# Rows of modes by way of DRAM instead of by identity products, and one slot per pair for the second weights

## The chip, the cores and the metric

One Trainium2 chip, of which the kernel uses one core. The core has TensorE (PE: matrix products into PSUM), VectorE (DVE), ScalarE (ACT), GpSimd (POOL) and SyncE (SP); POOL, SP and ACT can issue DMAs, and 16 DMA engines carry them. The metric is the device time of one execution in microseconds (us), lower is better.

## What is computed

Eight samples of 3264 positions with 192 channels. A causal convolution of seven taps per head comes first; its result, u0 here, is the input of a spectral layer that keeps the 64 lowest modes. Cut to what matters:

```python
def _attn_ref(x, weight):            # x (8, 3264, 192), weight (8 heads, 7)
    w = softmax(weight)              # over the taps
    return conv_per_head(zero_pad_left(x, 6), w)

def _moe_ref(x, w_r, w_i, w_ch):     # x: the result above
    X = np.fft.rfft(x, axis=1)
    Y[:, :64] = X[:, :64] @ (w_r + 1j * w_i)      # one 192x192 matrix per mode
    y = np.fft.irfft(Y, n=S, axis=1)
    u = x + y
    return u + np.maximum(u @ w_ch, 0.0)
```

## The kernel before

**First stage.** POOL's queue loads x, one pair of samples after the other (line 166, 177; float32 in DRAM, bf16 in SBUF), then w_ch (284, 286), then the weights of the modes in 16 groups of four modes (`load_w`, line 292), each group as two DMAs. Four pairs of samples q = 0 to 3 go through the convolution (`conv_pass`), a fold and a DFT as matrix products (`dft`), and a transpose of the spectrum (`xtrans`) to columns of modes, `xt`. The convolved rows stay in SBUF in `xall`; their transposes `ct` are made on the side (`trans_banks`).

**Mixing.** For each group g of four modes, `mix(g)` makes twelve products with the group's weights. Two groups make a step d = g // 2. `mix_copy(d)` copies the mixed spectrum of a step out of PSUM into one of two buffers `ymix`, in rows (mode of four, real or imaginary, sample). `mix_trans(d)` transposes it on PE and copies it to `yet`: 192 channels on partitions (128 and, a second time, the last 64), one column per mode and part, for each sample b. The last two groups have their own copies (lines 798 and 808), since everything after waits for them.

**Second stage.** For rows of modes, two things are wanted for each sample: the spectrum itself and the spectrum times w_ch. With those, the time signal is a product with a table `gtab` (modes by positions). Before, one set of products gives both, since the weight tiles `wa` and `wb` hold w_ch in their first 192 columns and an identity in the next 192: `yet` times that is 384 columns, spectrum times w_ch and spectrum. The result is scaled by `ascale` (2/S, and 1/S for mode 0) and kept in `zw[:, 0]` and `zw[:, 1]`. For the first pair of samples `zw_even` and `zw_odd` (lines 535 and 543) do this at once; for samples 2 to 7 each has a place in the list of slots.

The list of slots is the order of the second stage. An item (q, kk) is 256 positions of both samples of a pair; it has two slots, a = 0 and 1, of 128 positions. 52 items make 104 slots. A slot has one of eight PSUM banks (NZ = 8, slot s in bank s % 8) and goes through: C products (`ct` times w_ch, three of 192 columns on each half of the array's rows), a g product (`gtab` times `zw[:, 0]`, 384 columns on each half), a clamp at zero on ScalarE (`relu`, line 658), a y product (`gtab` times `zw[:, 1]`, 384 columns on each half) onto the clamped values, and an add of the convolved rows on VectorE (`finish`, line 679) into an output buffer. When both slots of an item are added, SP issues the store (line 699). Products that use 64 rows of the array run beside those of the other half; on one bank the halves take turns (`product`). A slot (None, b) is not an item: its products are those of the second weights of sample b, and `second_weights` (line 666) copies them to `zw`. The C products of the first five slots (`c_ahead`) and of ten others (`pairs`, "held" slots here) are made during the mixing; the held ones are parked in SBUF and brought back by ScalarE (`restore`, line 644).

**Order.** All orders of instructions are fixed when the program is built. `second_stage` (line 710) plays the stage through with assumed costs (`TAKES`, `TURN`, `SEEN`, `LOAD`) and writes PE's, ScalarE's and VectorE's instructions in the order that comes out.

**Output buffers.** `NO` buffers take the results of the first 16 items (`LATE`) in turn; six lie in `arena`, where weights lay before, and a seventh in `band`, the table of the convolution. Later items use six more in the part of `xall` that is done with. `relu` of an item waits for the stores of the item that had its buffer before (`before`, `wait_for`).

Of the kernel before, what the change touches and what calls it, by code (L numbers as in the profile page):

```python
# [19 lines left out]
def kernel(  # L20
# [9 lines left out]
    nc = tc.nc  # L30
# [58 lines left out]
    spare = sb("spare", [NK - 4, 2 * D], F32)  # L89
    ymix = [sb(f"ymix{i}", [2, D], BF16) for i in range(2)]  # L90
    bd3 = band[:, :].rearrange("p (h c) -> p h c", h=H)
    ctw = [ct[:, q, :, :, :].rearrange("p k t c -> p (k t c)") for q in range(NQ)]
# [7 lines left out]
    def wbuf(g):  # L100
# [137 lines left out]
    nc.vector.memset(ascale[:], 2.0 / S)  # L238
    nc.vector.memset(ascale[0:1, :], 1.0 / S)

# [35 lines left out]
    for u in units[6:8]:  # L276
        load_unit(*u)
    nc.gpsimd.memset(wa[:, D:2 * D], 0.0)
# [5 lines left out]
    nc.gpsimd.dma_start(out=wa[:, 0:D], in_=moe_w_ch[0:P, :])  # L284
    for i in range(2):
        nc.gpsimd.dma_start(out=wb[64 * i:64 * i + 64, 0:D], in_=moe_w_ch[P:D, :])


    NG = MODES // 4
    LAST = NG // 2 - 1  # L290

    def load_w(g):
        if g < NG:
            m0 = 8 * (g // 2) + g % 2
# [188 lines left out]
    def mix_bank(g):  # L483
        return sums[(g // 2 + (g == NG - 1)) % 2]

    def mix(g):
        yp = mix_bank(g)[:, D * (g % 2):D * (g % 2) + D]
        for j in range(3):
            for p4 in range(4):
                m = 8 * (g // 2) + g % 2 + 2 * p4  # L490
                nc.tensor.matmul(yp[32 * p4:32 * p4 + 2 * B, :], xt[:, j, :, m],  # L491
                                 wbuf(g)[:, p4, j, :], start=(j == 0), stop=(j == 2),
                                 tile_position=(0, 32 * p4), skip_group_check=True)
        if g >= NWC:
            load_w(g + NWA)

    def mix_copy(d):
        nc.scalar.copy(out=ymix[d % 2][:], in_=sums[d % 2][:, 0:2 * D].rearrange("p (g d) -> p g d", g=2))

    def mix_trans(d, groups=(0, 1), banks=None, parts=((0, B),)):  # L500

        ets = [((banks[t] if banks else ye[d % 2])[:, :].bitcast(BF16)[:, 2 * P * t:2 * P * (t + 1)]).rearrange(
            "p (g k) -> p g k", g=2) for t in range(2)]
        g0, ng = groups[0], len(groups)
        for t in range(2):
            for g in groups:
                nc.tensor.transpose(ets[t][:, g, :], ymix[d % 2][:, g, 64 * t:64 * t + P], ident[:])
        for b0, b1 in parts:
            for t in range(2):
                rows = slice(64 * t, P)  # L510
                dst = yet[rows, t, b0:b1, :].rearrange("p b (r c j) -> p r c b j", r=2, c=2)[
                    :, g0:g0 + ng, :, :, 4 * d:4 * d + 4]
# [9 lines left out]
    def scaled(dst, srcv, engine, rows=slice(0, P)):  # L522
        if engine == "v":
            return nc.vector.tensor_scalar(out=dst, in0=srcv, scalar1=ascale[rows, 0:1], scalar2=None, op0=ALU.mult)
        return nc.scalar.activation(out=dst, in_=srcv, func=ACT.Copy, scale=ascale[rows, 0:1])


    zfirst = ymix[(LAST + 1) % 2]

    def zw_part(o, i, t, modes=slice(0, P)):  # L530
        for k, w in enumerate((wa, wb)):
            nc.tensor.matmul(o, yet[:, k, i, modes], w[:, D * t:D * t + D], start=(k == 0),  # L532
                             stop=(k == 1), skip_group_check=True)

    def zw_even():

        r = slice(0, 64)
        o = ye[1][r, P:P + 2 * D]
        for i in range(2):
            zw_part(o[:, D * i:D * i + D], i, 0, r)  # L540
        scaled(zfirst[r, :, :], o.rearrange("p (i d) -> p i d", i=2), "a", r)

    def zw_odd():
        r = slice(64, P)
        w, y = (sums[0][:, 0:D], ye[0][:, 2 * P:2 * P + D]), ye[1][:, P:P + 2 * D]
        for i in range(2):
            zw_part(w[i], i, 0)
        for i in range(2):
            zw_part(y[:, D * i:D * i + D], i, 1)
        for i in range(2):  # L550
            scaled(zfirst[r, i, :], w[i][r, :], "av"[i], r)
        scaled(zw[:, 1, 0:2, :], y.rearrange("p (i d) -> p i d", i=2), "v")

# [31 lines left out]
    def pieces(s, row, which):  # L585
        n, a = slots[s]
        r = slice(64 * row, 64 * row + 64)
        if n is None:
            sides = ((0, wa),) if row == 0 else ((0, wa), (1, wb))
            return [(slice(0, 2 * D), yet[r, t, a, :], w[r, :]) for t, w in sides]  # L590
        q, kk = items[n]
        t = 2 * kk + a
        if which == "c":
            return [(slice(D * i, D * i + D), ct[r, q, blk, t, :], w[r, 0:D])
                    for blk, w, i in ((0, wa, 0), (1, wa, 1), (2, wb, row))]
        z = zw[r, 1 if which == "y" else 0, 2 * q:2 * q + 2, :] if q or which == "y" else zfirst[r, :, :]
        return [(slice(0, 2 * D), gtab[r, t, :], z.rearrange("p b d -> p (b d)"))]
# [68 lines left out]
    def second_weights(s, engine):  # L666
        q, i = divmod(slots[s][1], 2)
        copy = scaled(zw[:, :, 2 * q + i, :], Z[s % NZ][:, 0:2 * D].rearrange("p (t d) -> p t d", t=2), engine)
# [38 lines left out]
    HEAD = (-300, 330, 1500)  # L707
    TAKES = {"clamp": (930, 1150), "add": (1120, 1340), "copy": (1200, 1450), "restore": (950, 1200)}

    def second_stage():  # L710
# [30 lines left out]
        while left:  # L741
# [9 lines left out]
            if kind == 0:  # L751
# [5 lines left out]
                else:  # L757
# [6 lines left out]
            product(s, row, piece, row == 0 and k == 0 and s >= NC and slots[s] not in kept,  # L764
                    n is None and row == 1 and k == 1)
            free[row] = t + piece[0].stop - piece[0].start
# [7 lines left out]
            elif n is None:  # L774
                e = "a"
                second_weights(s, e)
# [17 lines left out]
    for g, beside in enumerate((0, 1, 1, 2, 2, 2, 1, 2, 2, 2, 2, 2, 2, 2, 0, 0)):  # L794
        d = g // 2
        mix(g)
        if g == NG - 2:
            nc.scalar.copy(out=ymix[d % 2][:, 0, :], in_=mix_bank(g)[:, 0:D])
            Z += hand_out("left", "out", (1, 1, 1, 1))
# [7 lines left out]
        elif g == NG - 1:  # L807
            nc.vector.tensor_copy(out=ymix[d % 2][:, 1, :], in_=mix_bank(g)[:, D:2 * D])  # L808
            g_ahead(range(2))
# [49 lines left out]
```

## Time and profile before

| | us |
|---|---|
| median of 3 runs (lowest, highest) | 176.18 (176.15, 177.23) |
| the profiled execution | 175.63 |
| its span, first to last instruction | 173.8 |
| busy in the span: PE | 149.3 (86%) |
| weight loads of PE | 126.5 (73%) |
| VectorE | 125.3 (72%) |
| ScalarE | 121.2 (70%) |
| GpSimd | 64.4 (37%) |

In the rows of the profile PE is the matrix product, PEld its weight load, SPq and POOLq the queues that issue DMAs. `outleft`, `sumright` and `mixright` are the PSUM banks of the second stage. A row of a group has the line of the kernel, engine, operation, output and inputs, the count, and durations. A row of the chain or of the timeline begins with its start and its length in us. A clamp is ScalarE at line 658, an add VectorE at line 679, a store SP at line 699. Of a DMA, "to landing" is the time from its issue until its data are there.

### The profile page before, as it was taken

The page shows a single profiled execution, that of the slowest core. Times are in us where ns is not written, and L with a number is a line of the kernel's source. Part 1 is how long each engine was busy: PE and PEld are TensorE (multiplying, and loading weights), DVE is VectorE, ACT ScalarE, POOL GpSimd, SP SyncE. Part 2 cuts the span into 40 slices and gives each one's busy share as a digit, 9 for nine tenths or more (in the row PEclk, how much of TensorE's full clock was granted, in tenths as well). Part 3 has the DMA queues.
Part 4 walks back from the last instruction along what each step waited for, and adds up shares of the span by engine and source line. Part 5 has one row for each costly group of instructions (what it writes and reads, how often), then busy time and mean ns, then how long its engine had stood idle before and what let it go on. Part 6 is the DMA issues. An engine that isn't in the chain of part 4 may idle for free.

```text
span 173.8 us, 6637 instructions
## 1 busy us (share of the span) xinstructions
PE 149.3 (86%) x2837; PEld 126.5 (73%) x2837; DVE 125.3 (72%) x244; ACT 121.2 (70%) x228; POOL 64.4 (37%) x106
## 2 busy tenths in 40 slices
PE   0043897899999998799998999999999999999980
PEld 0042796789889887677875754788999998999950
DVE  3892878466868868675555461597999998999990
ACT  6368365668686685665765663799989989988850
POOL 7977999877775474344244200000000000000000
PEclk9999699999999999999999999999999999999997
DMA  2999999999999999999999993088799999989995
GB/s 14 170 184 190 192 188 191 191 190 192 191 190 191 196 209 204 206 210 203 206 207 206 207 203 57 6 330 304 287 350 385 346 344 367 342 295 341 397 358 203
DMA packets 50594, 40.16 MB, mean 231 GB/s; under 512 B 29060, under 2 KB 50564, under 8 KB 50564
## 3 DMA queue, kind: packets, MB, share of 16 engines
q0 software_dynamic: 36208, 19.67, 82.3%
q1 hardware_dynamic: 14084, 19.87, 31.4%
q8 instruction: 22, 0.36, 0.8%
q10 hardware_dynamic: 272, 0.20, 0.3%
q14 instruction: 8, 0.07, 0.1%
HBM read 39.33 MB, written 20.05 MB: 342 GB/s over the span
## 4 chain that ended last, share of the span: by engine, by line
DMA 43%; PE 34%; POOL 15%; issue 3%; DVE 2%; POOLq 0%; DVEq 0%
DMA xall<-in_x_dram 18%; PE outleft L612 17%; DMA arena<-in_moe_w_i_dram 12%; DMA ct<-in_moe_w_i_dram 12%; POOL xall L166 11%; PE sumright L612 8%; PE mixright L612 8%; DVE arena L679 1%; POOL ct L296 1%; POOL loose L262 1%; PE sumright L491 1%; POOL wa L262 0%; POOL arena L296 0%; PE mixright L532 0%; DVE ymix L808 0%
## 5 line engine op out<-in xcount | busy, mean ns | idle before, releaser
L315 PEld LDWEIGHTS <-band 128*64 128x64 bf16 x944 | 38.0, 118 | 18.4 <-ACT band L233 11.0
L612 PEld LDWEIGHTS <-ct 64*128 64x128 bf16 x624 | 40.5, 94 | 5.9 <-PE trleft L612 0.5
L612 PE MATMUL outleft<-mixa,gtab 64*128 64x384 bf16 x186 | 41.9, 323 | 0.0
L315 PE MATMUL cvleft<-xall,band 128*64 128x192 bf16 (+4 forms) x640 | 29.9, 242 | 13.9 <-ACT band L233 11.0
L166 POOL DMA_DIRECT2D xall<-in_x_dram x48 | 35.9, 760 | 7.6 <-DMA xall<-in_x_dram 6.1
L612 PEld LDWEIGHTS <-gtab 64*128 64x128 bf16 x416 | 30.2, 94 | 3.4 <-PE sumright L612 0.9
L612 PE MATMUL outleft<-wa,ct 64*128 64x192 bf16 x196 | 29.9, 243 | 0.0
L344 DVE TENSOR_TENSOR arena<-xall 128x1536 bf16<-128x1536 bf16 (+1 forms) x28 | 22.4, 841 | 7.8 <-ACT xall L339 7.5
L339 ACT CAST xall<-cvleft 128x768 bf16<-128x768 f32 (+3 forms) x29 | 21.4, 756 | 9.1 <-PE cvleft L315 8.5
L658 ACT ACTIVATE outleft<-outleft 128x384 f32<-128x384 f32 x54 | 24.7, 475 | 3.3 <-PE sumright L612 0.8
L612 PE MATMUL sumright<-mixa,gtab 64*128 64x384 bf16 x88 | 26.2, 323 | 0.1
L612 PE MATMUL mixright<-mixa,gtab 64*128 64x384 bf16 x90 | 26.3, 322 | 0.0
L612 PE MATMUL outleft<-wb,ct 64*128 64x192 bf16 x98 | 21.7, 243 | 0.0
L391 DVE COPY ct<-trleft 128x1024 bf16<-128x1024 bf16 (+1 forms) x19 | 12.4, 662 | 12.1 <-PE trleft L422 7.2
L679 DVE TENSOR_TENSOR arena<-outleft,xall 128x384 f32<-128x384 f32 x35 | 18.5, 554 | 2.6 <-PE outleft L612 2.1
L315 PE MATMUL cvright<-xall,band 128*64 128x192 bf16 (+4 forms) x304 | 15.7, 245 | 2.1 <-DVE xall L337 1.5
L612 PE MATMUL mixright<-wa,ct 64*128 64x192 bf16 x96 | 17.0, 243 | 0.0
L389 ACT COPY ct<-trleft 128x1024 bf16<-128x1024 bf16 x13 | 13.2, 1013 | 4.6 <-PE trleft L419 2.5
L339 ACT CAST xall<-cvright 128x768 bf16<-128x768 f32 (+3 forms) x13 | 9.8, 751 | 7.9 <-PE cvright L315 5.5
L612 PE MATMUL sumright<-wa,ct 64*128 64x192 bf16 x84 | 14.8, 243 | 0.0
L419 PEld LDWEIGHTS <-xall 128*128 128x128 bf16 x208 | 11.7, 98 | 2.6 <-issue 0.3
L658 ACT ACTIVATE mixright<-mixright 128x384 f32<-128x384 f32 x25 | 11.8, 480 | 1.7 <-PE mixright L612 0.5
(146 smaller groups left out, 284.2 us busy)
## 6 DMA issues: line engine op xcount, KB each, us to landing
out_dram<-arena SPq DMA_DIRECT2D x25, 384.0 KB, 3.6
xall<-in_x_dram POOLq DMA_DIRECT2D x48, 192.0 KB, 7.6
out_dram<-xall SPq DMA_DIRECT2D x18, 384.0 KB, 4.1
ct<-in_moe_w_r_dram POOLq DMA_DIRECT2D x8, 288.0 KB, 9.8
ct<-in_moe_w_i_dram POOLq DMA_DIRECT2D x8, 288.0 KB, 10.5
arena<-in_moe_w_r_dram POOLq DMA_DIRECT2D x8, 288.0 KB, 9.8
arena<-in_moe_w_i_dram POOLq DMA_DIRECT2D x8, 288.0 KB, 10.7
out_dram<-band SPq DMA_DIRECT2D x4, 384.0 KB, 4.3
```

What stands on the lines that cost most here:

```text
L166: nc.gpsimd.dma_start(out=xall[:, q, t % 2, k:k + 4, :], in_=src)
L262: nc.gpsimd.affine_select(out=dst, in_=dst, compare_op=ALU.not_equal, fill=fill, base=base, pattern=pattern, channel_multiplier=1)
L296: nc.gpsimd.dma_start(out=wbuf(g)[64 * half:64 * half + 64, :, :, :], in_=src[m0:m0 + 7:2, :, :].rearrange("m (p j) e -> p m j e", j=3))
L315: nc.tensor.matmul(o, bd3[:, h, c0:c0 + P - 1:2], xall[:, q, t, ks:ks + n, GRP * h:GRP * h + GRP], start=(main and a == 0), stop=not main, ...
L339: nc.scalar.copy(out=dst, in_=srcv)
L344: nc.vector.tensor_tensor(out=cpm[:, r, :, 0:2 * nb, :], in0=src[:, :, :, 0, :], in1=src[:, :, :, 1, :], op=op)
L389: nc.scalar.copy(out=out, in_=in_)
L391: nc.vector.tensor_copy(out=out, in_=in_)
L419: nc.tensor.transpose(o, cv[:, blk, 0:P], ident[:])
L612: m = nc.tensor.matmul((Z[s % NZ] if bank is None else bank)[:, cols], l, r, start=start, stop=stop, skip_group_check=True)
L658: act = nc.scalar.activation(out=z, in_=z, func=ACT.Relu)
L679: add = nc.vector.tensor_tensor(out=o[:, :, a, :], in0=Z[s % NZ][:, 0:2 * D].rearrange("p (i d) -> p i d", i=2), in1=c_rows(q, kk)[:, a, : ...
```

## The change

- `mix_copy` and the copies of the last two groups scale at once, by 2/S, or by `ascale` for the group with mode 0; `ascale` is 1/S on the 16 rows of mode 0. They write all eight steps side by side into one buffer, `yall`, in the space of `band`; the two buffers `ymix` go.
- The steps are taken in another order, `md(d)`: 6, 7, 0, 1, 2, 3, 4, 5. The weights are loaded in that order.
- `y_rows`, new, after `zw_odd`: four DMAs on SP write the mixed spectrum from `yall` to a DRAM tile `yrows`, ordered by mode; four DMAs on POOL's queue read samples 2 to 7 back into `zy`, in rows of modes. `zy` takes the place of `zw[:, 1]`.
- The identity columns of `wa` and `wb` and the four POOL operations that made them go. `zw_odd` makes the first pair's rows of modes by products with `ident` (128 and 64 columns).
- What is left of the second weights, spectrum times w_ch, has one slot per pair: three slots with six products of 192 columns, instead of six slots with three products of 384. They stand at 11, 33 and 36 of the list (before: 12, 14, 17, 21, 68, 72). Their copies alternate between ScalarE and VectorE and do not scale.
- `NO` is 6: the output buffer in `band` goes.
- Other held slots: (18, 23), (30, 35, 43, 50), (58, 66, 74, 75), before (10, 17), (26, 30, 40, 47), (57, 63, 70, 76).

```diff
-    NO = 7
+    NO = 6
...
-    band = sb("band", [H * 2 * P], BF16)
+    band = sb("band", [max(H * 2 * P, MODES // 8 * 2 * D)], BF16)
...
-    zw = mixa[:, 0:2 * B * D].rearrange("p (t b d) -> p t b d", t=2, b=B)
-    wa = sb("wa", [2 * D], BF16)
-    wb = sb("wb", [2 * D], BF16)
+    zw, zy = [mixa[:, B * D * t:B * D * (t + 1)].rearrange("p (b d) -> p b d", b=B) for t in range(2)]
+    wa = sb("wa", [D], BF16)
+    wb = sb("wb", [D], BF16)
...
+    yall = band[:, :].rearrange("p (n g d) -> p n g d", g=2, d=D)
+    dram = ctx.enter_context(tc.tile_pool(name="dram", bufs=1, space=bass.MemoryType.DRAM))
+    yrows = dram.tile([MODES // 2, 2 * B, 2, D], BF16, tag="yrows", name="yrows")
...
-            [arena[:, OB * i:OB * (i + 1)] for i in range(NO - 1)] + [band[:, 0:OB]] +
+            [arena[:, OB * i:OB * (i + 1)] for i in range(NO)] +
...
-    nc.vector.memset(ascale[0:1, :], 1.0 / S)
+    nc.vector.memset(ascale[0:2 * B, :], 1.0 / S)
...
-    nc.gpsimd.memset(wa[:, D:2 * D], 0.0)
-    nc.gpsimd.memset(wb[:, D:2 * D], 0.0)
-    select(wa[:, D:2 * D], 1.0, 0, [[-1, D]])
-    select(wb[:, D:2 * D], 1.0, 64, [[-1, D]])
...
+    def md(d):
+        return (d + NG // 2 - 2) % (NG // 2)
...
     def mix_copy(d):
-        nc.scalar.copy(out=ymix[d % 2][:], in_=sums[d % 2][:, 0:2 * D].rearrange("p (g d) -> p g d", g=2))
+        srcv = sums[d % 2][:, 0:2 * D].rearrange("p (g d) -> p g d", g=2)
+        if md(d) == 0:
+            for g in range(2):
+                scaled(yall[:, md(d), g, :], srcv[:, g, :], g == 0, "a")
+        else:
+            scaled(yall[:, md(d), :, :], srcv, False, "a")
...
         for i in range(2):
-            zw_part(y[:, D * i:D * i + D], i, 1)
+            for k, cols in enumerate((slice(0, P), slice(P, D))):
+                nc.tensor.matmul(y[:, D * i + cols.start:D * i + cols.stop], yet[:, k, i, :],
+                                 ident[:, 64 * k:P], start=(i == 0 and k == 0), stop=True, skip_group_check=True)
...
+    def y_rows():
+        for p4 in range(4):
+            nc.sync.dma_start(out=yrows[p4:MODES // 2:4, :, :, :].rearrange("n k g d -> k n (g d)"),
+                              in_=yall[32 * p4:32 * p4 + 2 * B, :, :, :].rearrange("p n g d -> p n (g d)"))
+        for g in range(2):
+            for c in range(2):
+                r0 = 64 * g + 32 * c
+                nc.gpsimd.dma_start(out=zy[r0:r0 + 32, 2:B, :], in_=yrows[:, B * c + 2:B * c + B, g, :])
...
-    for k, b in zip((12, 14, 17, 21, 68, 72), range(2, B)):
-        slots.insert(k, (None, b))
+    for k, q in zip((11, 33, 36), range(1, NQ)):
+        slots.insert(k, (None, q))
...
-    for q, banks in ((0, (10, 17)), (1, (26, 30, 40, 47)), (2, (57, 63, 70, 76))):
+    for q, banks in ((0, (18, 23)), (1, (30, 35, 43, 50)), (2, (58, 66, 74, 75))):
...
-            return [(slice(0, 2 * D), yet[r, t, a, :], w[r, :]) for t, w in sides]
+            return [(slice(D * i, D * i + D), yet[r, t, 2 * a + i, :], w[r, :]) for i in range(2) for t, w in sides]
...
-                e = "a"
+                e = "va"[slots[s][1] % 2]
...
     zw_odd()
+    y_rows()
```

More of the change, by code (lines that the diff above doesn't have):

```diff
@@ L495, in mix, with scaled @@
             load_w(g + NWA)
-    def mix_copy(d):
-        nc.scalar.copy(out=ymix[d % 2][:], in_=sums[d % 2][:, 0:2 * D].rearrange("p (g d) -> p g d", g=2))
+    def scaled(dst, srcv, first, engine):
+        scale = ascale[:, 0:1] if first else 2.0 / S
+        if engine == "v":
+            return nc.vector.tensor_scalar(out=dst, in0=srcv, scalar1=scale, scalar2=None, op0=ALU.mult)
+        return nc.scalar.activation(out=dst, in_=srcv, func=ACT.Copy, scale=scale)
+    def mix_copy(d):
+        srcv = sums[d % 2][:, 0:2 * D].rearrange("p (g d) -> p g d", g=2)
[4 more added lines that the diff above has]
+            scaled(yall[:, md(d), :, :], srcv, False, "a")
     def mix_trans(d, groups=(0, 1), banks=None, parts=((0, B),)):
@@ L520, in mix_trans, with plain, zw_part @@
                     nc.scalar.copy(out=dst, in_=srcv)
[L522 to L530, printed above, removed]
+    def plain(dst, srcv, engine):
+        return nc.vector.tensor_copy(out=dst, in_=srcv) if engine == "v" else nc.scalar.copy(out=dst, in_=srcv)
+    def zw_part(o, b, modes=slice(0, P)):
         for k, w in enumerate((wa, wb)):
-            nc.tensor.matmul(o, yet[:, k, i, modes], w[:, D * t:D * t + D], start=(k == 0),
-                             stop=(k == 1), skip_group_check=True)
+            nc.tensor.matmul(o, yet[:, k, b, modes], w[:], start=(k == 0), stop=(k == 1), skip_group_check=True)
     def zw_even():
@@ L539, in zw_even @@
         for i in range(2):
[L540 to L541 removed]
+            zw_part(o[:, D * i:D * i + D], i, r)
+        plain(zfirst[r, :, :], o.rearrange("p (i d) -> p i d", i=2), "a")
     def zw_odd():
@@ L666, in second_weights @@
     def second_weights(s, engine):
-        q, i = divmod(slots[s][1], 2)
-        copy = scaled(zw[:, :, 2 * q + i, :], Z[s % NZ][:, 0:2 * D].rearrange("p (t d) -> p t d", t=2), engine)
+        q = slots[s][1]
+        copy = plain(zw[:, 2 * q:2 * q + 2, :], Z[s % NZ][:, 0:2 * D].rearrange("p (i d) -> p i d", i=2), engine)
         if engine == "v":
@@ L707 @@
     HEAD = (-300, 330, 1500)
-    TAKES = {"clamp": (930, 1150), "add": (1120, 1340), "copy": (1200, 1450), "restore": (950, 1200)}
+    TAKES = {"clamp": (930, 1150), "add": (1120, 1340), "copy": (960, 1200), "restore": (950, 1200)}
     def second_stage():
@@ L797 @@
         if g == NG - 2:
-            nc.scalar.copy(out=ymix[d % 2][:, 0, :], in_=mix_bank(g)[:, 0:D])
+            scaled(yall[:, md(d), 0, :], mix_bank(g)[:, 0:D], False, "a")
             Z += hand_out("left", "out", (1, 1, 1, 1))
@@ L807 @@
         elif g == NG - 1:
-            nc.vector.tensor_copy(out=ymix[d % 2][:, 1, :], in_=mix_bank(g)[:, D:2 * D])
+            scaled(yall[:, md(d), 1, :], mix_bank(g)[:, D:2 * D], False, "v")
             g_ahead(range(2))
```

28 lines of the change are left out of this document (14 added, 14 removed).

## The prediction

> **What bounds the kernel now.** I read the head of the page and its chain first, then busy time by stretches, then the chain in order of time around the joint between the two stages, and last the clamps and stores of the second stage.
>
> ```profile
> span 173.8 us, 6637 instructions
> DMA 43%; PE 34%; POOL 15%; issue 3%; DVE 2%; POOLq 0%; DVEq 0%
> ```
>
> DMA and POOL together are the first 58% of the chain, PE the rest. The stretches say why (columns: length, busy time of PE, weight loads, VectorE, ScalarE, GpSimd, clock, DMA share, GB/s):
>
> ```profile
> 8.00:10.00 2.00, 0.00 (x0) 0.00 (x0) 1.76 (x8) 0.96 (x2) 2.00 (x3) 1.00 1.53 179
> 102.00:104.00 2.00, 2.00 (x45) 1.23 (x39) 1.30 (x3) 1.47 (x3) 0.00 (x0) 1.00 1.20 205
> 106.00:108.00 2.00, 1.86 (x25) 0.79 (x23) 0.34 (x1) 0.58 (x1) 0.00 (x0) 1.00 0.10 16
> 108.00:110.00 2.00, 1.90 (x19) 1.34 (x21) 1.02 (x5) 0.68 (x3) 0.00 (x0) 1.00 0.00 0
> 112.00:113.00 1.00, 1.00 (x14) 0.57 (x10) 1.00 (x3) 1.00 (x4) 0.00 (x0) 1.00 0.03 8
> 113.00:119.00 6.00, 6.00 (x97) 5.10 (x97) 5.13 (x11) 5.73 (x14) 0.00 (x0) 1.00 0.93 349
> 160.00:166.00 6.00, 6.00 (x110) 5.55 (x108) 5.84 (x12) 4.93 (x12) 0.00 (x0) 1.00 1.01 372
> ```
>
> Up to 104 us the DMA engines are never free (share over 1, since packets overlap). From 106 to 113 they are idle: the last weights are in and no result is out. After 113 the stores fill them again, while PE and ScalarE are busy all the time. The joint in the chain of waits:
>
> ```profile
> 96.82 10.22 DMA arena<-in_moe_w_i_dram
> 107.08 0.49 PE sumright L491 x12
> 107.66 0.37 DVE ymix L808
> 108.99 0.49 PE mixright L532 x6
> ...
> 166.99 1.98 DVE arena L679 x4
> 168.99 0.56 DVE arena L679
> ```
>
> The last weight tile lands at 107.04; mixing, copying, transposing and the first pair's products follow one another until the first clamp at 110.2; then products bind until the last add at 169. PE's pace there can be read from ScalarE's clamps of the same two banks, one turn of the eight banks apart:
>
> ```profile
> 162.56 1.05 ACT L658 ACTIVATE sumright<-sumright 128x384 f32<-128x384 f32 x2
> 167.14 1.05 ACT L658 ACTIVATE sumright<-sumright 128x384 f32<-128x384 f32 x2
> ```
>
> Eight slots take 4.58 us, 0.573 us each. A slot streams 1344 columns through each half of the array (three C products of 192, one g and one y product of 384), so a column of one half costs 0.573/1344 = 0.426 ns.
>
> **The change, part by part.**
>
> *Second weights on PE.* Before, six slots hold three products of 384 columns each, one on the upper half of the array and two on the lower:
>
> ```profile
> L612 PE MATMUL sumright<-wa,yet x6: 322/322/323, 114.3 to 144.3; 64*128 64x384 bf16 x6
> L612 PE MATMUL sumright<-wb,yet x3: 323/323/323, 115.3 to 144.6; 64*128 64x384 bf16 x3
> ```
>
> After, three slots hold six products of 192. Per slot the columns are the same (384 above, 768 below, mean 576: 0.245 us), and there are three slots fewer: 3 x 0.245 = **0.74 us saved**. If only the upper half counted it would be 3 x 384 x 0.426 ns = 0.49, if the lower one 0.98. PE is busy to the end, so this lies on the path.
>
> *Their copies on ScalarE.* A scaled copy, a clamp, and (L498) a plain cast of the same size:
>
> ```profile
> 115.88 0.58 ACT L525 ACTIVATE mixa<-sumright,ascale 128x384 bf16<-128x384 f32 x1
> 116.36 0.48 ACT L658 ACTIVATE sumright<-sumright 128x384 f32<-128x384 f32 x1
> ...
> L498 ACT CAST ymix<-sumright x7: 479/480/484, 78.3 to 101.7; 128x384 bf16<-128x384 f32 x7
> ```
>
> Six of 0.58 become two of 0.48 here and one on VectorE: 2.5 us less on ScalarE, and the early held slots move from 10 and 17 to 18 and 23. ScalarE is no limit late (4.93 of 6 us) but nearly one in 113 to 119 (5.73 of 6). There PE issues 97 products where 160 to 166 has 110: at ten products per 0.573 us the 13 missing are worth 0.75 us at most. Part of the shortfall is only that the second products are wide and that held slots have no narrow ones. So 0 to 0.75; I take **0.15**, near zero.
>
> *The joint.* The first pair's products with the channel weights stay; its rows of modes now need 128 and 64 columns instead of twice 192, but they run beside the copies that the first g products wait for. Scaling moves from those copies to the mixing copy, which is on the path as well:
>
> ```profile
> 109.26 0.42 DVE L524 TENSOR_SCALAR ymix<-mixright,ascale 64x192 bf16<-64x192 f32 x1 [0.56 <-PE mixright L532]
> 107.66 0.36 DVE L808 CAST ymix<-sumright 128x192 bf16<-128x192 f32 x1 [1.91 <-PE sumright L491]
> ```
>
> One gets about 0.06 shorter, the other up to 0.06 longer: zero, with 0.1 either way. The other mixing copies get 0.10 longer each (0.58 against 0.48), and the one with mode 0 splits in two; that hides behind the weight stream (share 1.20). Uncovered it would be about 1 us. The new order of the weight tiles moves the same bytes.
>
> *GpSimd ahead of the loads.* Four operations that built the identity columns go:
>
> ```profile
> 27.51 0.34 POOL L278 MEMSET wa<- 128x192 bf16 x1
> ...
> 28.75 0.35 POOL L262 TENSOR_SCALAR_AFFINE_SELECT wb<-wb 128x192 bf16<-128x192 bf16 x1
> ...
> 52.37 0.54 POOL L284 DMA_DIRECT2D wa<-in_moe_w_ch_dram  x1 [0.27 <-DMA xall<-in_x_dram]
> ```
>
> That is 1.59 us of issuing time (27.51 to 29.10). The queue behind it is full and GpSimd later waits for it (the wait in the last row), so: zero.
>
> *The way through DRAM.* Four writes on SP and, when they have landed, four reads on GpSimd's queue. Prices, from stores:
>
> ```profile
> 112.78 5.21 SPq L699 DMA_DIRECT2D out_dram<-arena  x6
> 122.37 0.42 SPq L699 DMA_DIRECT2D out_dram<-arena  x1
> 127.92 0.45 SPq L699 DMA_DIRECT2D out_dram<-band  x1
> ...
> out_dram<-arena SPq DMA_DIRECT2D x1, 384.0 KB, 2.4
> out_dram<-band SPq DMA_DIRECT2D x1, 384.0 KB, 3.0
> ```
>
> The writes wait for VectorE's copy (108.02). Four issues of 0.42 end at 109.7; SP's next instruction, the first store, comes at 112.78, so nothing is held up. They land by 112.1 to 112.7, wholly in the idle stretch. Then GpSimd, with nothing else to do, issues four of 0.54 until about 114.6. The reads land by 117 to 118; if they took as long as the last weight tile did in a full queue (10.2), by 124.8. They are first wanted by the y product of item 13, the second item in the band buffer, stored at 127.92; its clamp starts at 124.61:
>
> ```profile
> 124.61 0.47 ACT L658 ACTIVATE mixright<-mixright 128x384 f32<-128x384 f32 x1
> ```
>
> Hence its y product waits until 125.1, and no wait shows there. What the reads do to the stores is another matter:
>
> ```profile
> q0 software_dynamic: 36208, 19.67, 82.3%
> q1 hardware_dynamic: 14084, 19.87, 31.4%
> ```
>
> A packet of q0 (543 bytes on average) takes 0.823 x 16 x 173.8 / 36208 = 63 ns of an engine, one of q1 (1411 bytes) 62 ns. The reads are 4 x 32 x 6 = 768 runs of 384 bytes: by bytes at 349/0.93 = 375 GB/s 0.79 us of all engines, by packets 768 x 63 / 16 = 3.0 us. They fall into 112.5 to 116, just as the stores fill the engines. I take 1.0, nearer to the bytes, since no row prices a lone run and part of it precedes the first store.
>
> *Six output buffers instead of seven.* The band buffer now holds the spectrum. The clamp of item n waits for the stores of item n-6 until item 15. In the trace of before, with stores landing 2.4 to 3.0 us after issue:
>
> ```profile
> 119.75 0.37 SPq L699 DMA_DIRECT2D out_dram<-band  x1
> ...
> 123.25 0.47 ACT L658 ACTIVATE sumright<-sumright 128x384 f32<-128x384 f32 x1
> 125.12 0.47 ACT L658 ACTIVATE outleft<-outleft 128x384 f32<-128x384 f32 x1
> ```
>
> Item 6 clamps at 116.36, item 0 landed at 112.78 + 2.4 = 115.2: 1.2 spare. Item 12 clamps at 123.25, item 6 landed at 122.75: 0.5 spare. Item 14 clamps at 125.12, item 8 landed at 125.4: 0.25 short. Behind a waiting clamp stand all later clamps and restores of ScalarE, and PE's y products wait for them. With stores late by 1.0 the stall is about 0.5 at item 12, some of it taken up by PE's lead: **0.4 lost**; bounds 0 and 3.0 - 0.5 = 2.5.
>
> *Sum.* -0.74 - 0.15 + 0.4 = **-0.49 us**. The profiled execution took 175.63 us (span 173.8 and 1.8 around it) and would take 175.1. The median of the runs, 176.18, is 0.55 higher; from it: 175.7.
>
> **Rivals.** *No stall, and ScalarE's relief counts.* For it: ScalarE 5.73 of 6 us busy where four of its copies stood. Against: PE's busy time shows no gap. It gives -0.98 - 0.6 = -1.6, 174.6.
>
> *The ring of six stalls in full (slower).* Mechanism: the 384-byte reads cost by the packet, push the stores of items 1 to 5 back by up to 3.0 us, and clamps 6 to 14 wait. It decides from a delay of about 1.4 us (0.5 spare plus 0.89 gained). At 2.7 the loss is 2.2, net +1.3: 177.5. For it: 63 ns whatever the packet's size. Against: 1.2 us spare in the first round, idle engines until 113. The Trainium skill, "DMA: Bandwidth & Descriptors", section Specifications, says that pieces under 512 bytes fall short of line rate, since they are read, changed and written back; by that rule the dear end, and this rival's time, would come true. The trace agrees so far as the equal 63 and 62 ns go. The same page, Queues, rings and completion order, has each DMA engine alternate between its queues packet by packet, which would put the reads between the stores rather than behind them; no run here shows both queues busy at once.
>
> *The round trip comes late.* If the reads land after 125.1, each microsecond late is one lost; the bound of 124.8 just spares it. At 2 us late: -0.89 + 2 = +1.1, 177.3.
>
> **How the numbers follow.** Forecast 0.55 (175.1 to 176.2), ScalarE's relief 0.2, the ring's stall 0.2, the late round trip 0.05. The range leaves out the far tails of both outer cases: 174.4 (all gains, -0.98 - 0.75) to 177.5. One per cent, about what a measurement of this kernel can tell from no change (its three runs spread by 0.6%), is 1.76 us. Under 174.4 lies the best of the relief and a piece of the forecast's tail, 0.14; over 177.9 the worst of the stall and the late trip, 0.12; within, 0.74.
>
> **What would show it.** Second products: eighteen of 192 columns, and the last add about 0.5 us earlier after the first clamp. The four writes within 108 to 113 and no store held up on SP. Clamps of items 6 to 15 that wait for "DMA out_dram" show the ring's price; without any, the gain is 0.9. Store landings over 4 us around 114 to 120 would show dear reads. It is wrong if PE's pace changes from 0.573, if the first clamp moves by more than 0.2, or if a y product waits for the reads.

## The result, and the profile after

The changed kernel takes 177.77 us (median of 7 runs, 177.5 to 179.05), the kernel before 176.15 (7 runs, 175.62 to 177.23). The ratio is 1.0105, 95% interval 1.0069 to 1.0140: slower by some 1.05%, where 0.3% faster was forecast, and just outside the range (177.5). The profiled execution took 177.5 us, its span 175.7. Ratios here leave disturbed executions out; in two experiments (`e5`, `e8`) it was the profiled one, so their traces are not read.

The head of the page after, with the shares of the chain by engine (those of before stand in the prediction):

```profile
span 175.7 us, 6638 instructions
DMA 47%; PE 27%; DVE 9%; POOL 9%; issue 4%; ACT 0%; POOLq 0%; DVEq 0%; ACTq 0%
```

Three spans of the trace add up to the whole: until the first clamp, from there to the end of the last add (the *stage*), from there to the end of the span (the *end*). The first clamp and the last add, after:

```profile
110.81 1.62 ACT L681 ACTIVATE outleft<-outleft 128x384 f32<-128x384 f32 x4 [0.75 <-PE outleft L635]
...
170.09 0.56 DVE L702 TENSOR_TENSOR arena<-sumright,xall 128x384 f32<-128x384 f32 x1
```

| us | first clamp | stage | end |
|---|---|---|---|
| before | 110.20 | 59.34 | 4.28 |
| after | 110.81 | 59.84 | 5.07 |

All three grew. The first is scatter: the last weight landed at 107.04 us before and at 107.76 after, and from there to the first clamp it took 3.17 before and 3.06 after. By the prediction's sum the stage should have become 0.49 shorter; it became 0.50 longer. The windows show where: five of them after (columns as in the prediction), then the three that answer in the trace of before.

```profile
114.00:118.00 4.00, 4.00 (x77) 3.59 (x74) 3.72 (x9) 3.27 (x8) 2.28 (x4) 1.00 0.87 299
116.00:118.00 2.00, 2.00 (x40) 1.81 (x36) 1.72 (x5) 1.98 (x6) 0.79 (x2) 1.00 0.88 277
118.00:122.00 4.00, 3.75 (x65) 3.16 (x61) 3.19 (x7) 3.02 (x8) 0.00 (x0) 1.00 1.06 392
122.00:126.00 4.00, 3.48 (x54) 2.71 (x51) 2.88 (x6) 2.71 (x7) 0.00 (x0) 1.00 0.98 366
160.00:166.00 6.00, 6.00 (x110) 4.82 (x108) 5.85 (x12) 4.93 (x12) 0.00 (x0) 1.00 1.06 390
```

```profile
114.00:118.00 4.00, 4.00 (x67) 3.42 (x65) 3.72 (x9) 3.88 (x9) 0.00 (x0) 1.00 1.07 398
116.00:118.00 2.00, 2.00 (x37) 1.82 (x34) 1.72 (x5) 2.00 (x5) 0.00 (x0) 1.00 1.06 396
122.00:126.00 4.00, 4.00 (x73) 3.63 (x69) 3.62 (x8) 3.69 (x10) 0.00 (x0) 1.00 0.84 308
```

From 114 to 118 the changed kernel makes 77 products against 67 (some of them narrower). From 122 to 126 it makes 54 against 73, with PE, ScalarE and VectorE all idle for a while. Late in the stage PE's pace is the same as before (110 products in six us; the row of before stands in the prediction). What ended that idle time stands in the chain in order of time:

```profile
118.83 1.03 DVE arena L702 x2
119.88 4.60 DMA out_dram<-arena
124.56 0.48 ACT outleft L681
125.09 0.32 PE outleft L635
```

The add of item 6, its store, the clamp of item 12 behind that store, and PE behind the clamp: the ring of six. Two earlier turns of it, as rows of SP's timeline, the DMA view (last number: us from issue to landing) and ScalarE's timeline:

```profile
115.33 0.37 SPq L722 DMA_DIRECT2D out_dram<-arena  x1
117.29 0.37 SPq L722 DMA_DIRECT2D out_dram<-arena  x1
...
out_dram<-arena SPq DMA_DIRECT2D x1, 384.0 KB, 4.5
out_dram<-arena SPq DMA_DIRECT2D x1, 384.0 KB, 5.3
...
119.95 1.25 ACT L681 ACTIVATE outleft<-outleft 128x384 f32<-128x384 f32 x3 [0.85 <-PE outleft L635]
122.67 0.47 ACT L681 ACTIVATE sumright<-sumright 128x384 f32<-128x384 f32 x1 [0.70 <-PE sumright L635]
```

Item 2's store is issued at 115.33 and lands at 119.86; item 8 clamps at 119.95. Item 4's, issued at 117.29, lands at 122.58; item 10 clamps at 122.67. The profile puts both waits down to PE, but a clamp that begins 0.08 us after a landing, twice, and the same for items 11 and 12, waits for the landing. In the trace of before the same two stores, issued at 114.68 and 116.56, landed 2.6 and 2.9 us after issue:

```profile
out_dram<-arena SPq DMA_DIRECT2D x1, 384.0 KB, 2.6
...
out_dram<-arena SPq DMA_DIRECT2D x1, 384.0 KB, 2.9
```

The way through DRAM, after:

```profile
108.84 1.89 SPq L570 DMA_DIRECT2D yrows<-band  x4
...
114.51 2.28 POOL L575 DMA_DIRECT2D mixa<-yrows  x4 [16.17 <-PE mixright L635]
...
yrows<-band SPq DMA_DIRECT2D x4, 96.0 KB, 3.3
mixa<-yrows POOLq DMA_DIRECT2D x4, 72.0 KB, 3.9
```

The writes landed until 113.9, so the reads were issued from 114.51, in the midst of the first stores. Their packets, 192 of them in all, moved between 116.3 and 120.5. They took 24.8% of the 16 engines' time in these 4.2 us, 1.04 us of all engines:

```profile
q0 software_dynamic: 192, 0.30, 24.8%
```

### The profile page after: what moved, and what is told of

It reads as the page before. It is cut to its first block, busy times and chain, and to the rows that moved or that the text cites. A ratio compares the mean times of both kernels' runs of the same rounds, so it can differ in the third digit from the quotient of the medians.

```text
span 175.7 us, 6638 instructions
## 1 busy us (share of the span) xinstructions
PE 149.8 (85%) x2837; PEld 125.8 (72%) x2837; DVE 124.9 (71%) x245; ACT 118.9 (68%) x225; POOL 65.2 (37%) x106
## 4 chain that ended last, share of the span: by engine, by line
DMA 47%; PE 27%; DVE 9%; POOL 9%; issue 4%; ACT 0%; POOLq 0%; DVEq 0%; ACTq 0%
DMA xall<-in_x_dram 22%; PE outleft L635 13%; DMA arena<-in_moe_w_i_dram 12%; DMA ct<-in_moe_w_i_dram 11%; POOL xall L170 7%; PE sumright L635 6%; DVE arena L702 5%; PE mixright L635 5%; DVE xall L702 4%; DMA out_dram<-arena 3%; PE sumright L494 1%; PE trleft L425 1%; POOL loose L266 1%; PE sumright L808 0%; PE mixright L522 0%
## 5 line engine op out<-in xcount | busy, mean ns | idle before, releaser
L318 PEld LDWEIGHTS <-band 128*64 128x64 bf16 x944 | 38.8, 121 | 18.6 <-ACT band L237 11.0
L318 PE MATMUL cvleft<-xall,band 128*64 128x192 bf16 (+4 forms) x640 | 30.5, 248 | 14.0 <-ACT band L237 11.0
L635 PEld LDWEIGHTS <-gtab 64*128 64x128 bf16 x416 | 29.5, 94 | 3.8 <-PE outleft L635 1.0
L635 PE MATMUL outleft<-wa,ct 64*128 64x192 bf16 x204 | 30.4, 243 | 0.0
L635 PE MATMUL sumright<-mixa,gtab 64*128 64x384 bf16 x88 | 25.4, 323 | 0.3 <-ACT sumright L681 0.2
L635 PE MATMUL mixright<-mixa,gtab 64*128 64x384 bf16 x92 | 25.5, 323 | 0.0
L635 PE MATMUL outleft<-wb,ct 64*128 64x192 bf16 x102 | 23.0, 243 | 0.0
L702 DVE TENSOR_TENSOR arena<-outleft,xall 128x384 f32<-128x384 f32 x37 | 19.7, 553 | 3.2 <-PE outleft L635 3.0
L635 PE MATMUL mixright<-wa,ct 64*128 64x192 bf16 x88 | 15.3, 242 | 0.0
L635 PE MATMUL sumright<-wa,ct 64*128 64x192 bf16 x84 | 13.9, 243 | 0.0
```

What stands on the lines that cost most here:

```text
L318: nc.tensor.matmul(o, bd3[:, h, c0:c0 + P - 1:2], xall[:, q, t, ks:ks + n, GRP * h:GRP * h + GRP], start=(main and a == 0), stop=not main, ...
L635: m = nc.tensor.matmul((Z[s % NZ] if bank is None else bank)[:, cols], l, r, start=start, stop=stop, skip_group_check=True)
L702: add = nc.vector.tensor_tensor(out=o[:, :, a, :], in0=Z[s % NZ][:, 0:2 * D].rearrange("p (i d) -> p i d", i=2), in1=c_rows(q, kk)[:, a, : ...
```

## The experiments

Each begins from the changed kernel, unless it says otherwise. Times move by some tenths between sessions, so ratios to the kernel before, run in the same session, are compared.

**Seven buffers** (`e1_ring7`): the spectrum in `band` is dead once it is written out, so the seventh buffer goes there.

```diff
-    NO = 6
+    NO = 7
...
-            [arena[:, OB * i:OB * (i + 1)] for i in range(NO)] +
+            [arena[:, OB * i:OB * (i + 1)] for i in range(NO - 1)] + [band[:, 0:OB]] +
```

> The changed kernel (177.77 us) with seven output buffers again: the seventh lies in the band space, over the spectrum that the four writes to DRAM have read by then. If the clamps of items 8, 10, 11 and 12, which begin 0.08 us after the store of the item six before has landed, are the cause, they wait no longer, PE's idle time between 120 and 126 us (some 1.5 us) goes, and the time is 176.3 (176.0 to 176.7). If PE's stall comes from the new order of the slots, or from the DMA traffic in another way, nothing changes: 177.5 to 178.0.

Measured: 177.29 us, ratio 1.0064 (1.0038 to 1.0091). Less than half of the loss went. The stage took 59.55, and clamps of items 11 and 12 still began 0.08 us after the landing of the item seven before. Neither expectation held: by the trace the ring is a cause, but with these stores seven are too few as well.

**Without the DMAs** (`e2_noroute`), six buffers:

```diff
-    y_rows()
+    nc.gpsimd.memset(zy[:, 2:B, :], 0.0)
```

> The changed kernel with six buffers, but the eight DMAs by way of DRAM left out; the rows of modes of samples 2 to 7 are set to zero instead, so their mixed spectrum is missing from the output. If the ring stalls only because the reads push the stores back by some 2 us, the first stores land 2.4 to 2.9 us after issue as before, no clamp waits for one by more than 0.3 us, and the time is 176.3 (176.0 to 176.7). If six buffers are too few on their own, it stays at 177.3 or above.

Measured: 176.73 us, ratio 1.0027 (1.0001 to 1.0054). The stage took 58.60 us, and the stores of items 2, 4 and 5 landed 2.8, 3.1 and 3.8 us after issue (4.5, 5.3 and 5.0 in the changed kernel). Item 12 alone still waited for a store, 0.4 us; the rest of the stall was gone. So the DMAs make the stores late and the ring turns it into a stall. The time stayed above the expected band because the end grew to 5.86.

**Longer runs in DRAM** (`e3_longruns`):

```diff
-    yrows = dram.tile([MODES // 2, 2 * B, 2, D], BF16, tag="yrows", name="yrows")
+    yrows = dram.tile([MODES // 8, 2, 4, 2 * B, D], BF16, tag="yrows", name="yrows")
...
-                nc.gpsimd.dma_start(out=zy[r0:r0 + 32, 2:B, :], in_=yrows[:, B * c + 2:B * c + B, g, :])
+                nc.gpsimd.dma_start(out=zy[r0:r0 + 32, 2:B, :].rearrange("p b d -> p (b d)"),
+                                    in_=yrows[:, g, :, B * c + 2:B * c + B, :].rearrange("n p k d -> n p (k d)"))
```

> The changed kernel with another layout of the DRAM tile: the writes are 1024 runs of 384 bytes (before 512 of 768), the reads 128 runs of 2304 bytes (before 768 of 384). If the reads cost by the run (63 ns each, 3.0 us of all engines), they cost 0.8 us now, the stores of items 2 to 5 land some 2 us earlier, and the time falls to 176.6 (176.2 to 177.0). If they cost by the byte, it stays at 177.5 to 178.0.

Measured: 177.61 us, ratio 1.0096 (1.0061 to 1.0131): unchanged, and the sixth store landed 5.0 us after issue, as in the changed kernel. The price is not that of short runs. The trace shows the reads as 192 packets here too. The writes, now in runs of 384 bytes, landed 2.6 to 4.1 us after issue, against 2.5 to 4.0.

**The last held slots as before** (`e4_heldend`):

```diff
-    for q, banks in ((0, (18, 23)), (1, (30, 35, 43, 50)), (2, (58, 66, 74, 75))):
+    for q, banks in ((0, (18, 23)), (1, (30, 35, 43, 50)), (2, (57, 63, 70, 76))):
```

> The changed kernel with the last held slots at (57, 63, 70, 76) as before, not (58, 66, 74, 75). In the changed kernel the last add belongs to item 49, whose store is one of 384 KB that lands 4.2 us after issue; here the last add is item 51's, whose two halves go out separately. If that end costs what the two traces show (last add to the end of the span 5.6 us against 4.8), the time is 177.0 (176.7 to 177.3). If the end is set by stores already queued, it stays at 177.5 to 178.0.

Measured: 177.64 us, ratio 1.0085 (1.0049 to 1.0122): 0.2% less than the changed kernel, not clear of the noise. In the trace the end is 4.60 against 5.07. The expectation had the stores wrong in one point: item 49 is a short item, stored in two pieces of 144 KB. After the last add at 170.09, SP's timeline of the changed kernel has them one behind the other:

```profile
170.68 0.83 SPq L722 DMA_DIRECT2D out_dram<-arena  x2
```

**Both, without the DMAs** (`e5_noroute_end`: the edits of `e2` and `e4`):

> The kernel without the eight DMAs (samples 2 to 7 lack their mixed spectrum in the output) and with the last held slots at (57, 63, 70, 76). Without the DMAs alone the stage from first clamp to last add took 58.6 us, 0.74 less than before, but from the last add to the end of the span 5.9 us, 1.6 more than before. If that end belongs to the order of the last slots (item 49 last, with one store of 384 KB), it falls to some 4.5 us and the time to 175.6 (175.2 to 176.0), under the kernel before. If the end is a backlog of stores that any faster stage meets, the time stays at 176.5 to 177.0.

Measured: ratio 0.9985 (0.9955 to 1.0015), 0.42% under `e2`. The uncertainty of that difference is 0.40%, so it is only just clear of the noise. Together with the shorter end in the trace of `e4` it says that the held slots are a cost of their own.

**Seven buffers and the held slots, with the DMAs** (`e6_ring7_end`: the edits of `e1` and `e4`):

> The changed kernel with its DMAs, with seven buffers (the seventh in the band space) and the last held slots at (57, 63, 70, 76). Seven buffers gave 177.29, the held slots 177.64, from 177.77. If the two are separate costs they add up: 177.1 (176.8 to 177.4). If the end only shows what the ring has delayed, the second brings nothing on top: 177.3 or more.

Measured: 177.24 us, ratio 1.0037 (1.0005 to 1.0068). The time lies where separate costs would put it, but by ratio it is 0.27% under `e1`, within the noise; the end is 4.71 in its trace, against 5.19 in that of `e1`. One stall is left, at item 12, whose clamp begins 0.08 us after item 5's store has landed (123.37). In ScalarE's timeline:

```profile
121.27 1.05 ACT L681 ACTIVATE mixright<-mixright 128x384 f32<-128x384 f32 x2
123.45 1.78 ACT L681 ACTIVATE outleft<-outleft 128x384 f32<-128x384 f32 x4 [1.13 <-DMA out_dram<-arena]
```

**Six buffers in the kernel before** (`e7_before_six`):

```diff
-    NO = 7
+    NO = 6
...
-            [arena[:, OB * i:OB * (i + 1)] for i in range(NO - 1)] + [band[:, 0:OB]] +
+            [arena[:, OB * i:OB * (i + 1)] for i in range(NO)] +
```

> The kernel before with six output buffers instead of seven, nothing else. If six buffers alone are too few, clamps of items 12 to 15 wait for stores and the time rises from 176.2 to 177 or more. If it takes the reads to make them too few, only items 13 and 14 wait, by 0.3 us, and the time is 176.2 to 176.5.

Measured: 176.41 us, ratio 0.9981 (0.9954 to 1.0008): no cost. The stage took 59.35 against 59.34. Its waits (in all, times, longest) name one store:

```profile
ACT outleft L658 <- DMA out_dram<-arena: 0.3, 1, 0.3
```

That is item 14, for which the prediction had read a shortage of 0.25 us; ScalarE makes it up.

**An earlier way through DRAM** (`e8_early`, with the edits of `e6`):

```diff
-        return (d + NG // 2 - 2) % (NG // 2)
+        return d
...
-            zw_even()
+            y_rows(0, LAST, zw_even())
...
-    y_rows()
+    y_rows(LAST, LAST + 1)
+    y_back(0, LAST)
+    y_back(LAST, LAST + 1)
```

`y_rows(n0, n1, after)` writes the steps n0 to n1, here behind the copy in `zw_even`; `y_back(n0, n1)` issues the reads of their rows.

> As with seven buffers and the held slots at (57, 63, 70, 76), but the way through DRAM starts earlier: the steps are taken in the order of the modes, the first seven of eight are written once the copy of the first pair's even modes is done (about 107 us), the last one after its own copy, and the reads of the first seven (28 of 32 mode rows) are issued ahead of those of the last. If the reads cost because they come at 114.5, when the stores have begun, they are issued at about 111 now and mostly land before 114; the stores land 2.4 to 3.2 us after issue and the time is 176.0 (175.6 to 176.4). If the reads hurt wherever they are, or delay the last weights, it stays at 177.0 or above.

Measured: ratio 1.0044 (1.0013 to 1.0075), no better than `e6`. The same kernel again for its trace (`e10_early_again`):

> The kernel with the early way through DRAM once more, for its trace. If the early writes push back the last weights, the first clamp comes 3.5 us or more after the last weight has landed instead of 3.1. If the reads still meet the stores, stores land 4 us or more after issue between 114 and 120. If neither, the stage is below 59 us and the loss lies in the end.

```profile
112.20 4.79 POOL L578 DMA_DIRECT2D mixa<-yrows  x8 [14.25 <-PE outleft L636]
...
out_dram<-arena SPq DMA_DIRECT2D x1, 384.0 KB, 5.3
```

The first clamp came 3.04 us after the last weight, as in the changed kernel (3.06): nothing was pushed back there. But the writes of the first seven steps, issued from 107.4, landed only at 111.6, eight reads take GpSimd until 117.0 to issue, and the stores around them still landed over 5 us after issue (the row is the one at 118). Stage 59.26. The second branch held; reads that are over before the stores begin were not reached this way.

**Without the DMAs, with seven buffers and the held slots** (`e9_noroute_end_ring7`):

> Without the eight DMAs (samples 2 to 7 lack their mixed spectrum in the output), with seven buffers and the last held slots at (57, 63, 70, 76). What is left of the change is PE's shorter second weights and ScalarE's fewer copies, with no clamp waiting for a store in the first sixteen items. If PE's pace sets the end, the stage takes 58.5 us or less against 59.34, the end after the last add 4.3 to 4.6, and the time is 175.5 (175.2 to 175.9). If the stores' own pace sets the end, the stage is shorter but the last store lands as before and the time is 176.0 to 176.4.

Measured: 175.80 us, ratio 0.9957 (0.9926 to 0.9988). The stage took 58.41 us, no clamp waited for a store, and PE kept its pace through the window that was empty in the changed kernel:

```profile
122.00:126.00 4.00, 4.00 (x73) 3.89 (x70) 3.78 (x9) 3.75 (x10) 0.00 (x0) 1.00 0.98 359
```

In its one trace, of the slowest of its twelve executions (176.93 us), the end is 5.3 us, longer by about as much as the stage is shorter, with the last stores landing 3.6 to 4.0 us after issue against 2.9 to 3.4. Time says 0.4% gained, the trace says that part of PE's gain is given back to the stores; how much, one trace does not tell. Against `e5`, the same with six buffers, it is 0.28% less, within the noise: that six cost anything without the DMAs is not shown.

**Both kernels again, for their traces** (`e11_changed_again`, `e12_before_again`):

> The changed kernel once more, for a second trace. If the first clamp at 110.8 (before 110.2) is only a scatter of the load stream, it lies anywhere between 110.0 and 111.3 here; the stage from first clamp to last add takes 59.8 again, the end 5.1.

> The kernel before once more, for a second trace. If the load stream scatters whatever the kernel, the first clamp lies between 110.0 and 111.3; the stage takes 59.3 again, the end 4.3.

```profile
111.66 1.62 ACT L681 ACTIVATE outleft<-outleft 128x384 f32<-128x384 f32 x4 [0.75 <-PE outleft L635]
```

```profile
110.69 1.62 ACT L658 ACTIVATE outleft<-outleft 128x384 f32<-128x384 f32 x4 [0.77 <-PE sumright L612]
```

The first clamp of the changed kernel came at 111.66 this time, that of the kernel before at 110.69, with six buffers at 111.20, and that of `e6` at 110.12. Both kinds lie between 110.1 and 111.7, and it is the last weight that scatters: from its landing to the first clamp it took 3.17 to 3.18 us in the three traces with the old first stage, and 3.04 to 3.09 in the twelve with the changed one. So the 0.6 us between the first two traces is no cost of the change. The stage of the kernel before repeated exactly (59.34). That of the changed kernel was longer, 60.69, not the 59.8 expected: clamps waited 1.8 us for stores by name, and that one execution took 179.44 us. The stall itself varies.

**Reads split by pair** (`e13_bypair`, with the edits of `e6`): the second pair's reads at once, the others behind the adds of items 15 and 24.

```diff
+    y_back(1)
...
+        if n in (15, 24):
+            y_back({15: 2, 24: 3}[n], added[n, a])
```

`y_back(q)` issues the four reads of pair q alone.

> Seven buffers and the last held slots at (57, 63, 70, 76), and the reads split by pair of samples: those of the second pair as soon as the writes have landed, those of the third and fourth pair only after the add of item 15 and of item 24, when thirteen buffers are in turn. If the whole cost of the way through DRAM (177.24 against 175.80 without it) is that 295 KB of reads at 114 us push the first stores back by more than the ring has to spare, a third of them does not reach the clamps: no clamp waits for a store, the stage takes 58.4 to 58.7 us, the time is 175.8 (175.4 to 176.2), under the kernel before. If any read at that place stalls the stores, or the later ones cost as much, it stays at 176.8 to 177.3.

Measured: 176.28 us, ratio 0.9981 (0.9952 to 1.0010), 0.56% under `e6` by the same buffers and held slots. Stage 58.66. No wait stands under a store's name, but item 12's clamp began 0.08 us after the landing of item 5's store (122.55), after 0.29 us of idle time; it is the only one. From the window and the DMA view:

```profile
122.00:126.00 4.00, 4.00 (x69) 3.43 (x65) 3.73 (x8) 3.48 (x9) 0.00 (x0) 1.00 0.97 341
...
out_dram<-arena SPq DMA_DIRECT2D x1, 384.0 KB, 4.7
```

The sixth store still lands late (4.7 us; 3.7 in `e9`, 5.5 in `e6`), but nearly within what seven buffers allow. The later reads cost nothing that shows in the stage; the end took 5.5 us, as long as in `e9` (5.3) without any reads. It is the best version with a complete output; from the kernel before it cannot be told apart.

**Reads on SP** (`e14_onsp`, with the edits of `e6`):

```diff
-                nc.gpsimd.dma_start(out=zy[r0:r0 + 32, 2:B, :], in_=yrows[:, B * c + 2:B * c + B, g, :])
+                nc.sync.dma_start(out=zy[r0:r0 + 32, 2:B, :], in_=yrows[:, B * c + 2:B * c + B, g, :])
```

> Seven buffers, held slots at (57, 63, 70, 76), all four reads issued by SP behind the writes instead of by GpSimd. SP then waits for the writes (about 113.9) ahead of the first store, which leaves 1.5 to 2.5 us late. If GpSimd's queue makes the reads dear (2 to 2.5 us of delay for 0.75 us of data), the stores land within 3.5 us of issue and the time is 177.0 or below; if the reads themselves do, the stores land 4 us or more after issue on top of the late start: 177.8 or above.

```profile
113.94 1.75 SPq L575 DMA_DIRECT2D mixa<-yrows  x4
115.81 4.73 SPq L722 DMA_DIRECT2D out_dram<-arena  x6
```

Measured: 178.08 us, ratio 1.0063 (1.0030 to 1.0096). SP stood until the writes had landed, so the first store left at 115.8 instead of 112.7, and the stores of items 3 to 6 landed 5.2 to 5.7 us after issue. Slower than `e6` by 0.26%, within the noise of both. The late landings fit the second branch, but not for its reason: the reads were issued ahead of all stores, and from 117 on the DMA engines moved as much as without reads (the row below), so this is the backlog of stores that began late and close together. Whether GpSimd's queue is what makes the reads dear is therefore not tested.

```profile
117.00:122.00 5.00, 4.59 (x80) 3.74 (x78) 3.81 (x9) 3.90 (x10) 0.00 (x0) 1.00 1.06 391
```

**Reads split by pair, six buffers** (`e15_bypair_six`):

> The reads split by pair as above, held slots at (57, 63, 70, 76), but with six buffers as in the changed kernel. If six buffers cost only together with the reads, a third of the reads delays the stores by about 0.7 us, within the 0.9 to 1.4 us that six buffers have to spare in the first turn: 176.3 (175.9 to 176.7). If six buffers have no room for any delay, 177.2 or above.

Measured: 177.37 us, ratio 1.0033 (1.0004 to 1.0061), 0.5% over `e13`, with an uncertainty of 0.4%. The waits of its ScalarE:

```profile
ACT mixright L683 <- DMA out_dram<-arena: 1.0, 1, 1.0
...
ACT outleft L683 <- DMA out_dram<-arena: 0.5, 1, 0.5
```

Six buffers have no room even for a third of the reads.

## Why the prediction was wrong

What failed is the term for the six buffers behind the way through DRAM: +0.4 in the sum, some 2.2 us measured. A second cost, of some 0.4 us at the end of the kernel, was no term at all. By steps along the ratios (1% is 1.76 us), the first with an uncertainty of 0.3%, the others of 0.4 to 0.5%: from the kernel before to `e9` -0.43% (-0.8 us), the DMAs added at seven buffers (`e9` to `e6`) +0.80% (+1.4 us), six buffers for seven (`e6` to `e4`) +0.48% (+0.8 us), the last held slots moved (`e4` to the changed kernel) +0.20% (+0.4 us). The sum is +1.05%. The step for the DMAs is clear of the noise; that for the buffers is at its edge and rests on the traces as well (the clamps' waits, and `e13` against `e15`).

- **Second weights on PE, -0.74.** Held. Without the DMAs the stage took 58.60 and 58.41 us for 59.34 (-0.74 and -0.93), and in `e9` the time fell by 0.8.
- **ScalarE's relief, -0.15.** Not seen apart from the former; together they were forecast at 0.89 and measured in the stage at 0.74 to 0.93. The rival that made it 0.6 fell.
- **The joint and GpSimd's four operations, 0.** Held: the last weight scatters over 1.5 us and shows no shift, and from there to the first clamp it is 0.1 us shorter, at the edge of what the prediction allowed.
- **The way through DRAM.** This step failed in its times. The prediction let the writes land by 112.1 to 112.7, with the 2.4 to 3.0 us of a store of 128 partitions. They start from 16 partitions each and landed 2.5 to 4.0 us after issue, the last at 113.9. So the reads were issued at 114.5, not 112.4, and none of them fell ahead of the stores. Of the two prices the upper one had the count wrong: the reads are 192 packets, not 768, and took 1.04 us of all engines, not 3.0. The 1.0 that was taken is near that, but it is not what the stores lose: they landed some 2 us later than before (1.2 to 2.2 later than in `e2`), and with runs six times as long it was the same. That the y products of item 13 would not wait was right; no wait of PE for the reads shows in any trace.
- **Six buffers, +0.4.** The mechanism was right, with its clamps, but the term was mis-sized, being the sum of a delay of 1.0 and a spare of 0.5. Measured were 1.4 for the DMAs at seven buffers and 0.8 more at six. Without the DMAs six cost nothing in the kernel before, as the spare read there (1.2 us at item 6, 0.5 at item 12, 0.25 short at item 14) said. What the term overlooked is that the delay stays: two slots of 0.573 us make an item of 384 KB, 343 GB/s, and stores alone moved 398 (114 to 118, before), so a backlog of 2 us does not drain within a turn of the ring, and seven buffers meet it as well.
- **The held slots.** Their move was priced only for ScalarE's early load. At the end it puts a slot of item 49 behind item 51, so that the special store of the last item no longer ends the kernel: 0.2 to 0.4% by ratio in three pairs, one of them just clear of the noise, 0.5 us of the end in two pairs of traces (`e4`, `e6`), and no term of the sum.

The rival that the ring stalls in full came true as a stall and nearly in its time (177.5 forecast, 177.77 measured). Its reason was refuted, so the near hit in time is luck: the reads took 1.04 us of the engines, not 3.0, they do not cost by the run (`e3`), and some 0.4 us of the loss come from the held slots. From `e3` it also followed that the Trainium skill's rule on pieces under 512 bytes ("DMA: Bandwidth & Descriptors", Specifications) is not what decides here: reads in runs of 2304 bytes cost what runs of 384 bytes did. The writes, whose runs `e3` brought under 512 bytes, landed no later (113.8 us).

Settled in part is why the reads cost the stores more than their bytes, 295 KB, which at the stores' 398 GB/s is 0.74 us. While they run, the DMA engines move less and are less busy than without them, as the windows from 116 to 118 show: share 0.88 and 277 GB/s, against 1.06 and 396 before (393 in `e2` and in `e9`). The windows from 114 overstate it, since the first store left 0.66 us later. In the middle of item 2's store there is a stretch, 116.65 to 117.20, in which only packets of the reads were under way:

```profile
DMA packets 39, 0.06 MB, mean 116 GB/s; under 512 B 25, under 2 KB 25, under 8 KB 39
q0 software_dynamic: 39, 0.06, 60.9%
```

They held the engines for 61% of that time and moved 116 GB/s; in `e6` (114.85 to 115.35) it was 92% and 118 GB/s. So a packet of these reads holds its engine long for its bytes. For what it waits there, no run here tells.

## What to carry to other kernels

A transfer put into an idle stretch of the DMA engines must be timed with its slowest hop, from rows of its own shape: a write from 16 partitions did not land like a store from 128. If the reads that follow it fall among stores, what counts is how long the buffers behind those stores can wait, and at a pace near the DMA engines' own (343 of 398 GB/s here) a delay lasts for the whole ring. So read a ring's spare time clamp by clamp (landing of the last user against the next use) before shortening it, and split a read by when its parts are needed.

## What the runs showed of the hardware that was not expected

- Four writes of 96 KB, each from 16 partitions, landed 2.5 to 4.0 us after issue with the DMA engines otherwise idle, in runs of 768 bytes and of 384 alike (`e3`); the first store of 384 KB, from 128 partitions, landed in 2.4.
- Reads of 295 KB among stores cut what the DMA engines moved from 396 to 277 GB/s over two us, while their own packets took 1.04 us of all engines, and a third of them still delayed the sixth store by 1.0 us (4.7 against 3.7), the whole by 1.8 (5.5).
- The clamps' waits for landings stand in the profile mostly under PE's name; only the 0.08 us between landing and clamp gave them away.
